# A state-space scan followed by hash-routed experts: squares, inter-chunk products and routing placed differently in the turns of the scan

## The chip, the cores and the metric

The kernel runs on one core of a Trainium2 chip. Its time is the device time of one launch in microseconds (us). The core has five instruction streams that run beside each other and meet at semaphores: TensorE (PE in the profile, with its weight loads as PEld), VectorE (DVE), ScalarE (ACT), GpSimd (POOL) and SyncE (SP), which here only issues DMAs.

## The reference

Two stages. The first is a state-space scan over 4 batches, 8 heads and 768 positions with head width 32 and state width 16. With `L[i, j]` the decay from position j to position i, a chunk gives

```python
CB = np.einsum('bhin,bhjn->bhij', Cc, Bc)
M = CB * L                                   # L is causal
y_intra = np.einsum('bhij,bhjd->bhid', M, xc)
y_inter = np.einsum('bhin,bhnd->bhid', Cc, state) * decay_to_i[:, :, :, None]
y[:, :, sl] = y_intra + y_inter
...
state = decay_full[:, :, None, None] * state + np.sum(Bx, axis=2)
```

`Bx` is the product of B and x, decayed to the chunk's end. The result is laid out as 3072 tokens of width 256. In the second stage each token goes to one of 8 experts, chosen by `token_ids * 2654435761 % 8`, and gets `relu(x @ w1[e]) @ w2[e]` with a hidden width of 1024.

## The kernel before

Everything is in fp32 except the small one-hot tables. The order of instructions on every engine is the order of the program text; a tile framework only adds the waits.

**The scan.** The kernel uses chunks of 64 positions. Two blocks of 128 positions make a pair; there are 3 pairs per batch and 12 pairs in all (`NP`), numbered `k`, with `b, j = divmod(k, 3)`. The main loop (L724) runs `k` from -1 to 11; a pass is called a turn here. A turn works on several pairs at once:

- *Rows* (`rows_part`, L203, called by `rows_due`, L707): POOL multiplies B or C of a batch by decay factors. A batch has 6 blocks of B rows and 6 of C rows.
- *Squares* (`turn_bc`, L214): TensorE transposes these 128x128 blocks into PSUM, four in a turn: B 0 to 3, then B 4, 5 and C 0, 1, then C 2 to 5 (`PARTS`, L212). `evict_bc` (L225) copies them out as `bt` (from B) and as `ct` and two masked forms `ce` (from C), nearly all on ACT.
- *Back* (`back`, L520; `evict_back`, L526): two blocks of `bt` for pair k+2 are turned back into `bn`.
- *States* (`states`, L543): DVE carries the state `z` through the four chunks of pair k+1; POOL scales each state into `sp` (L553).
- *Inter* (`inter`, L591): TensorE adds C times state to the output of pair k in PSUM (16 matmuls, 12 where the pair opens a batch); ACT copies the finished output to `y_sb` (L609), and `y_store` (L626) issues two DMAs to a DRAM buffer `y_tokens` on SP.
- *Gram* (`gram`, L566): C times B for pair k+2 into PSUM banks 0 to 3; `masked` (L578): DVE copies the causal part to `m_sb`, in two halves.
- *Intra* (`intra`, L611): the masked matrices times x for pair k+1; at its end ACT reads one column of the two output banks into `seen` (L622).
- *Dstates* (`dstates`, L530): B times x for pair k+2, into the other halves of banks 0 and 1, from where DVE's `z` reads them.

[...] `BT` = 6 and `BQ` = 7 take squares and back, `BY` = 4 and 5 the outputs.

**The routing.** In turns 0 to 8, `piece(k)` (L675) runs a part of the routing between gram and the masked copies: counts, ranks and slots of the tokens per expert, mostly small operations on DVE and POOL (`rt_...`, L269 to L426). In turn 6 and 7 one-hot `laneoh` rows are made (`rt_lanes`, L403), in turn 8 TensorE multiplies them by a table (`rt_table`, L419), into columns 256 on of bank `BQ`, and `to_index` (L428) makes the indices by which tokens are gathered.

**The experts.** POOL gathers tokens from `y_tokens` by indirect DMA (`gather`, L474) in tiles of 128; `turn_x` (L482) transposes a tile on TensorE and copies it to `xT`. The first tiles are gathered in turns 8 to 10, and two of them (`AHEAD`, L717) are transposed in turn 10 (L750). After the loop the experts run in pairs of halves with a Strassen-like scheme: `sums_x`, `sum_w1` and `sum_w2` form sums of tokens and weights on DVE, `up` (L844) and `down` (L907) are the matmuls, `put` (L942) transposes a result and scatters it to the output by indirect DMA on POOL. Four experts' first products are made (L979 to L1003) before the steps of L1090. Weights come by DMAs that SP issues, the first of them in turns 3 to 10 (`LOADS`, L720).

Of the kernel before, what the change touches and what calls it, by code (L numbers as in the profile page):

```python
# [9 lines left out]
F32 = mybir.dt.float32  # L10
# [15 lines left out]
def kernel(  # L26
# [187 lines left out]
    def turn_bc(b, part, bank):  # L214
        if part == 0:
            bts[b] = abat.tile([P, S], F32, name="bt")
            cts[b] = abat.tile([P, S], F32, name="ct")
            ces[b] = abat.tile([P, 2, S], F32, name="ce")
        k = 0
        for i, r0, r1 in PARTS[part]:  # L220
            for r in range(r0, r1):
                pe.transpose(out=ps[:, bank, k * P:(k + 1) * P], in_=rows[b, i][:, r], identity=ident)  # L222
                k += 1

    def evict_bc(b, part, bank, eng):  # L225
        k = 0
        for i, r0, r1 in PARTS[part]:
            src = ps[:, bank, k * P:(k + r1 - r0) * P].rearrange("q (r p) -> q p r", p=P)
            k += r1 - r0
            outs = [(bts[b], None, 0)] if i == 0 else [(ces[b][:, 0], 0, 1), (ces[b][:, 1], 1, 2), (cts[b], None, 3)]  # L230
            for o, e, n in outs:
                if n >= len(eng) or eng[n] is None:
                    continue
                o = o.rearrange("q (p r) -> q p r", r=R)[:, :, r0:r1]
                if eng[n] is act:
                    act.activation(o, src, AF.Copy, scale=1.0 if e is None else par[:, e:e + 1])  # L236
                elif e is None:
                    dve.tensor_copy(out=o, in_=src)
                else:
                    dve.tensor_scalar(out=o, in0=src, scalar1=par[:, e:e + 1], scalar2=None, op0=OP.mult)  # L240
# [84 lines left out]
    def rt_placed(pick, who):  # L325
        dve.tensor_reduce(out=sel, in_=pick, axis=AX.X, op=OP.add)
        whof = small("whof", [P, E])
        dve.tensor_reduce(out=whof, in_=who, axis=AX.X, op=OP.add)
        dve.tensor_copy(out=place_i, in_=whof)
# [9 lines left out]
    def rt_over_b():  # L339
        ov_i = small("ov_i", [P, E], I32)  # L340
        dve.tensor_scalar(out=ov_i, in0=ov, scalar1=0.0, scalar2=float(P - 1), op0=OP.max, op1=OP.add)
        dve.tensor_scalar(out=ov_i, in0=ov_i, scalar1=P.bit_length() - 1, scalar2=None, op0=OP.logical_shift_right)
# [82 lines left out]
    def rt_tabled():  # L425
        dve.tensor_copy(out=tabacc.rearrange("q i k -> q (i k)"), in_=ps[:, BQ, 2 * P:2 * P + 2 * NK])  # L426
# [753 lines left out]
```

## Time and profile before

| | |
|---|---|
| median of 3 timed runs | 247.5 us (247.07 to 250.94) |
| the profiled execution | 238.82 us |
| its span, first to last instruction | 237.1 us, mean granted TensorE clock 0.99 |
| busy share of the span | PE 94%, PEld 86%, DVE 72%, POOL 42%, ACT 41% |
| the scan ends: first expert matmul (L865) | 68.10 us |

The profile comes from one execution. The page gives busy time by engine, the chain of waits that ended last, and the costliest groups of instructions; the trace behind it can be asked for a timeline of one engine or for busy time in chosen windows. In a timeline, a line gives the start and the length in us, the engine, the source line, the operation, output and inputs, shapes, how many instructions are merged, and in brackets how long the engine idled before it and what released it. Where an instruction waited for several things, the trace names the one that came last by its records, which can be the wrong one. PEld overlaps PE: [...].

The page's slices (40 of equal length, busy share in tenths) show how the load shifts from the scan to the experts:

```profile
PE   7989999998899999999999999999999999999980
PEld 5777777777689897999999999999999999998960
DVE  6688887986526699989899797676758749537520
ACT  3647446642336632214223326434625533543220
POOL 2477879796855772004303532101430420310441
```

### The profile page before, as it was taken

The page shows a single profiled execution, that of the slowest core. Times are in us where ns is not written, and L with a number is a line of the kernel's source. Part 1 is how long each engine was busy: PE and PEld are TensorE (multiplying, and loading weights), DVE is VectorE, ACT ScalarE, POOL GpSimd, SP SyncE. Part 2 cuts the span into 40 slices and gives each one's busy share as a digit, 9 for nine tenths or more (in the row PEclk, how much of TensorE's full clock was granted, in tenths as well). Part 3 has the DMA queues.
Part 4 walks back from the last instruction along what each step waited for, and adds up shares of the span by engine and source line. Part 5 has one row for each costly group of instructions (what it writes and reads, how often), then busy time and mean ns, then how long its engine had stood idle before and what let it go on. Part 6 is the DMA issues. An engine that isn't in the chain of part 4 may idle for free.

```text
span 237.1 us, 6843 instructions
## 1 busy us (share of the span) xinstructions
PE 222.7 (94%) x2695; PEld 205.0 (86%) x2695; DVE 170.1 (72%) x351; ACT 97.2 (41%) x249; POOL 100.1 (42%) x177
## 2 busy tenths in 40 slices
PE   7989999998899999999999999999999999999980
PEld 5777777777689897999999999999999999998960
DVE  6688887986526699989899797676758749537520
ACT  3647446642336632214223326434625533543220
POOL 2477879796855772004303532101430420310441
PEclk9999999999999999999999999999999999999995
DMA  7988987887857999106607528306011400610111
GB/s 170 208 142 171 190 190 168 182 181 184 251 156 178 277 284 366 45 0 214 231 0 249 195 70 257 141 3 195 30 47 45 167 28 5 198 44 3 46 46 48
DMA packets 55174, 33.23 MB, mean 140 GB/s; under 512 B 34986, under 2 KB 49474, under 8 KB 55140
## 3 DMA queue, kind: packets, MB, share of 16 engines
q1 hardware_dynamic: 52288, 26.09, 42.4%
q0 software_dynamic: 2400, 6.43, 8.4%
q8 instruction: 22, 0.36, 0.6%
q10 hardware_dynamic: 452, 0.25, 0.4%
q14 instruction: 12, 0.10, 0.2%
HBM read 26.47 MB, written 6.42 MB: 139 GB/s over the span
## 4 chain that ended last, share of the span: by engine, by line
PE 44%; issue 31%; POOL 9%; DVE 7%; DMA 3%; ACT 3%; POOLq 1%; DVEq 0%; ACTq 0%
PE ps L865 12%; PE ps L924 10%; POOL out_dram L953 9%; PE ps L618 5%; PE ps L574 3%; PE ps L603 3%; PE ps L175 3%; PE ps L222 2%; DMA xg<-y_tokens,idx_in 2%; PE ps L538 2%; ACT ce L236 2%; PE ps L485 1%; DVE s L806 1%; DMA y_tokens<-y_sb 1%; DVE m L582 1%
## 5 line engine op out<-in xcount | busy, mean ns | idle before, releaser
L953 POOL DMA_INDIRECT out_dram<-o_sb,idx_out x25 | 29.7, 1190 | 73.8 <-ACT o_sb L949 71.5
L477 POOL DMA_INDIRECT xg<-y_tokens,idx_in x25 | 26.5, 1060 | 41.8 <-PE ps L944 30.4
L865 PE MATMUL ps<-t,s 128*128 128x202 f32 (+7 forms) x192 | 38.0, 328 | 0.6 <-DVE u L893 0.4
L924 PE MATMUL ps<-t,s 128*128 128x202 f32 (+7 forms) x192 | 35.2, 326 | 0.0
L865 PEld LDWEIGHTS ps<-t,s 128*128 128x128 f32 x192 | 32.0, 189 | 1.7 <-DVE u L893 0.9
L924 PEld LDWEIGHTS ps<-t,s 128*128 128x128 f32 x192 | 31.3, 189 | 0.0
L865 PE MATMUL ps<-xT,w 128*128 128x202 f32 (+7 forms) x128 | 25.3, 329 | 0.0
L806 DVE TENSOR_TENSOR s<-w 128x512 f32<-128x512 f32 x32 | 21.9, 684 | 0.2 <-DMA w<-in_moe_w_dram 0.2
L865 PEld LDWEIGHTS ps<-xT,w 128*128 128x128 f32 x128 | 21.0, 189 | 0.7 <-ACT p1e L876 0.5
L898 ACT ACTIVATE hx<-hx 128x404 f32<-128x404 f32 (+7 forms) x16 | 8.3, 525 | 31.2 <-DVE hx L897 31.2
L553 POOL TENSOR_TENSOR sp<-z,gm 128x128 f32<-128x128 f32 x44 | 17.9, 424 | 3.8 <-DVE z L561 1.9
L582 DVE COPY_PREDICATED m<-cmask,ps 128x512 f32<-128x512 int32 x24 | 16.2, 728 | 2.8 <-PE ps L574 2.7
L563 DVE SCALAR_TENSOR_TENSOR z<-z,g_sb,ps 128x128 f32<-128x128 f32 x40 | 13.9, 347 | 4.9 <-PE ps L538 1.1
L618 PEld LDWEIGHTS ps<-x_t,m 64*64 64x64 f32 x768 | 12.6, 134 | 2.5 <-ACT y_sb L609 1.2
L618 PE MATMUL ps<-x_t,m 64*64 64x64 f32 x768 | 14.3, 221 | 0.2
L930 ACT ACTIVATE d<-ps 128x202 f32<-128x202 f32 (+7 forms) x24 | 8.0, 331 | 14.0 <-PE ps L924 13.9
L865 PE MATMUL ps<-t,w 128*128 128x202 f32 (+7 forms) x64 | 13.2, 330 | 0.4
L865 PE MATMUL ps<-xT,s 128*128 128x202 f32 (+7 forms) x64 | 12.9, 326 | 0.0
L603 PE MATMUL ps<-sp,ct 64*64 64x128 f32 x176 | 12.2, 276 | 0.4 <-ACT seen L622 0.4
L924 PE MATMUL ps<-t,w 128*128 128x202 f32 (+8 forms) x72 | 12.4, 314 | 0.0
L924 PE MATMUL ps<-h,w 128*128 128x202 f32 (+7 forms) x64 | 11.8, 326 | 0.0
L865 PEld LDWEIGHTS ps<-t,w 128*128 128x128 f32 x64 | 10.7, 189 | 1.2 <-DVE hx L897 1.2
(176 smaller groups left out, 439.2 us busy)
## 6 DMA issues: line engine op xcount, KB each, us to landing
w<-in_moe_w_dram SPq DMA_DIRECT2D x8, 1024.0 KB, 5.8
w<-in_moe_w_dram SPq DMA_DIRECT2D x11, 512.0 KB, 6.9
x_t<-in_x_dram SPq DMA_DIRECT2D x24, 128.0 KB, 4.3
y_tokens<-y_sb SPq DMA_DIRECT2D x23, 128.0 KB, 3.5
w<-in_moe_w_dram SPq DMA_DIRECT2D x10, 256.0 KB, 3.7
bc<-in_B_dram SPq DMA_DIRECT2D x4, 384.0 KB, 4.9
bc<-in_C_dram SPq DMA_DIRECT2D x4, 384.0 KB, 5.4
xg<-y_tokens,idx_in POOLq DMA_INDIRECT x25, 4.9
```

What stands on the lines that cost most here:

```text
L477: pool_e.indirect_dma_start(out=xg[k], out_offset=None, in_=y_dram[0:n, :], in_offset=bass.IndirectOffsetOnAxis(ap=idx_in[:, k:k + 1], axi ...
L553: pool_e.tensor_tensor(out=sps[k][:, n].rearrange("q (h d) -> q h d", d=D), in0=zs["z"].rearrange("q (h d) -> q h d", d=D), in1=gm[:, un - ...
L563: dve.scalar_tensor_tensor(out=z, in0=zs["z"], scalar=g_sb[:, un - 1:un], in1=d, op0=OP.mult, op1=OP.add)
L582: dve.copy_predicated(out=m[:, :, g], mask=mk, data=ps[:, g, 0:2 * P].rearrange("q g (t s) -> q t g s", t=2))
L603: pe.matmul(out=y_own(r, u)[:, t], lhsT=cts[b][r, c:c + T], rhs=sps[k][r, n], start=False, stop=True, skip_group_check=True)
L618: pe.matmul(out=o, lhsT=m_sb[k % 2][u * T:(u + 1) * T, t, h // 2, (h % 2) * T:(h % 2 + 1) * T], rhs=xs[2 * k + t][u * T:(u + 1) * T, h // ...
L806: dve.tensor_tensor(out=t[:, i], in0=a, in1=b, op=op)
L865: pe.matmul(out=ps[:, bank, i * n:(i + 1) * n], lhsT=lhs[:, (q0 + i) * P:(q0 + i + 1) * P], rhs=rhs, start=((what in (1, 5) or what == (6 ...
L898: act.activation(hq(2), hq(2), AF.Relu)
L924: pe.matmul(out=src, lhsT=lhs(q), rhs=rhs(q)[:, c0:c1], start=((what in (1, 5) or alone) and q == 0), stop=True, skip_group_check=True)
L930: act.activation(st[what], src, AF.Copy)
L953: st = pool_e.indirect_dma_start(out=out[:], out_offset=bass.IndirectOffsetOnAxis(ap=idx, axis=0), in_=o_sb, in_offset=None, bounds_check= ...
```

## The change

1. **Squares.** From batch 2 on, a batch's six B squares are turned in one turn and its six C squares in the next (turns 2 and 3 for batch 2, 5 and 6 for batch 3), the last two of each six into bank `BQ`, columns 256 on; turns 4 and 7 turn none. Turns -1 to 1 are as before. The rows are made by POOL in the same turns as before. All copies stay on ACT (two of the prologue's stay on DVE); in turns 3 and 6 the C copies stand behind `bn`, one of them behind `seen`, and one in the next turn.
2. **Inter** of turns 2 to 11 moves to the front of the turn, before squares and back.
3. **AHEAD**: the two first token tiles are turned at the head of turn 11 instead of within turn 10, and DVE copies them instead of ACT.
4. **Scalings**: `sp` of pairs 10 and 11 is made on DVE, each before the next `z`, instead of on POOL.
5. **Table**: in bank `BT` instead of `BQ`, where `bn` comes from.
6. **Routing**: `rank_a`, `rank_b` and lanes 0 to 4 go behind the masked copies of their turns; lanes 21 to 23 go from POOL to DVE; the expert numbers come from the reduction directly, without a cast; the shift takes its count from a tile.
7. **sums_x(0)** is called one `up` earlier, ahead of `sum_w1`'s last piece.

```diff
-    def turn_bc(b, part, bank):
...
+    def turn_bc(b, i, r0, r1, bank, k=0):
...
+        for r in range(r0, r1):
+            pe.transpose(out=ps[:, bank, (k + r - r0) * P:(k + r - r0 + 1) * P], in_=rows[b, i][:, r], identity=ident)
+
+    def evict_bc(b, i, r0, r1, bank, k, eng, n=0):
+
+        src = ps[:, bank, k * P:(k + r1 - r0) * P].rearrange("q (r p) -> q p r", p=P)
+        o, e = (bts[b], None) if i == 0 else (cts[b], None) if n == 2 else (ces[b][:, n], n)
...
@@ rt_placed
-        whof = small("whof", [P, E])
-        dve.tensor_reduce(out=whof, in_=who, axis=AX.X, op=OP.add)
-        dve.tensor_copy(out=place_i, in_=whof)
+        with nc.allow_low_precision("whole numbers below 8"):
+            dve.tensor_reduce(out=place_i, in_=who, axis=AX.X, op=OP.add)
@@ rt_over_b
-        dve.tensor_scalar(out=ov_i, in0=ov_i, scalar1=P.bit_length() - 1, scalar2=None, op0=OP.logical_shift_right)
+        dve.tensor_tensor(out=ov_i, in0=ov_i, in1=shift_i, op=OP.logical_shift_right)
@@ rt_table (and the same in rt_tabled)
-        o = ps[:, BQ, 2 * P:2 * P + 2 * NK]
+        o = ps[:, BT, 0:2 * NK]
@@ states
-                pool_e.tensor_tensor(out=sps[k][:, n].rearrange("q (h d) -> q h d", d=D),
+                (pool_e if k < NP - 2 else dve).tensor_tensor(out=sps[k][:, n].rearrange("q (h d) -> q h d", d=D),
@@ piece
-            rt_rank_a()
...
-            rt_rank_b()
...
-            rt_lanes(0, 5, dve)
             rt_lanes(18, 21, pool_e)
...
-            rt_lanes(21, NCH, pool_e)
@@ before the main loop
+    SQUARES = {-1: [(1, 0, 0, 4, BY + 1, 0)], 0: [(1, 0, 4, 6, BT, 0), (1, 1, 0, 2, BT, 2)], 1: [(1, 1, 2, 6, BT, 0)]}
+    for b in range(2, NB):
+        SQUARES[3 * b - 4] = [(b, 0, 4, 6, BQ, 2), (b, 0, 0, 4, BT, 0)]
+        SQUARES[3 * b - 3] = [(b, 1, 4, 6, BQ, 2), (b, 1, 0, 4, BT, 0)]
@@ main loop
-        bt_, part = (b + 2, 0) if j == 2 else (b + 1, j + 1)
-        tb, qb, sb = (BY + 1, BY, BT) if k == -1 else (BT, BQ, 0)
-        if bt_ < NB:
-            turn_bc(bt_, part, tb)
+        qb, sb = (BY, BT) if k == -1 else (BQ, 0)
+        if k == NP - 1:
+            for i, q in enumerate(AHEAD):
+                turn_x(q, (BQ, BT)[i % 2], dve)
+        sq = SQUARES.get(k, ())
+        soon = k > 1
+        if soon:
+            inter(k)
+        for q in sq:
+            turn_bc(*q)
         if k + 2 < NP:
             back(k + 2, qb)
         if k + 1 < NP:
             states(k + 1, (0, 1), sb)
-        if bt_ < NB and part == 0:
-            evict_bc(bt_, part, tb, (act,))
-        elif bt_ < NB:
-            evict_bc(bt_, part, tb, (act, act, None if part == 1 else act, None))
+        for q in sq:
+            if q[1] == 0:
+                evict_bc(*q, act)
+            elif not soon:
+                evict_bc(*q, act, 0)
+                if k == 1:
+                    evict_bc(*q, act, 1)
         if k + 1 < NP:
             states(k + 1, (2, 3), sb)
-        if k == NP - 2:
-            for i, q in enumerate(AHEAD):
-                turn_x(q, (BQ, BT)[i % 2])
-        if k >= 0:
+        if not soon and k >= 0:
             inter(k)
         if k + 2 < NP:
             evict_back(k + 2, qb)
...
-        if bt_ < NB and part > 0:
-            evict_bc(bt_, part, tb, (None, None, act if part == 1 else None, act))
+        for q in sq:
+            if q[1] == 1:
+                for n in ((1, 2) if k == 0 else (2,) if k == 1 else (0, 1, 2) if q[4] == BQ else (0,)):
+                    evict_bc(*q, act, n)
+        if k - 1 in (3, 6):
+            evict_bc(*SQUARES[k - 1][1], act, 2)
...
         if k + 2 < NP:
             masked(k + 2, 0)
             masked(k + 2, 1)
+        if k == 1:
+            rt_rank_a()
+        if k == 3:
+            rt_rank_b()
         if k == 5:
             rt_slot_e()
+        if k == 6:
+            rt_lanes(0, 5, dve)
         if k == 7:
             rt_lanes(13, 18, dve)
+            rt_lanes(21, NCH, dve)
         if k + 1 < NP:
             intra(k + 1)
+        if k in (3, 6):
+            evict_bc(*sq[1], act, 1)
         if k + 2 < NP:
             dstates(k + 2)
...
@@ first products of the experts
+                if n == 15:
+                    sums_x(0)
...
     assert not turns
-    sums_x(0)
```

More of the change, by code (lines that the diff above doesn't have):

```diff
@@ L212 @@
     PARTS = [[(0, 0, 4)], [(0, 4, 6), (1, 0, 2)], [(1, 2, 6)]]
-    def turn_bc(b, part, bank):
[L215 to L240, printed above, removed]
+    def turn_bc(b, i, r0, r1, bank, k=0):
+        for d, e in ((bts, 1), (cts, 1), (ces, 2)):
+            if b not in d:
+                d[b] = abat.tile([P, S] if e == 1 else [P, 2, S], F32, name=("bt", "ct", "ce")[(bts, cts, ces).index(d)])
+        for r in range(r0, r1):
[3 more added lines that the diff above has]
+        o, e = (bts[b], None) if i == 0 else (cts[b], None) if n == 2 else (ces[b][:, n], n)
+        o = o.rearrange("q (p r) -> q p r", r=R)[:, :, r0:r1]
+        if eng is act:
+            act.activation(o, src, AF.Copy, scale=1.0 if e is None else par[:, e:e + 1])
+        elif e is None:
+            dve.tensor_copy(out=o, in_=src)
+        else:
+            dve.tensor_scalar(out=o, in0=src, scalar1=par[:, e:e + 1], scalar2=None, op0=OP.mult)
     sh = [P, E, NCH]
@@ L366, in rt_rank_b @@
                           in1=shift.unsqueeze(2).to_broadcast([P, E, NCH - EARLY]), op=OP.add)
+    shift_i = apre.tile([P, E], I32)
+    dve.memset(shift_i, P.bit_length() - 1)
     def rt_half2():
@@ L425, in rt_tabled @@
     def rt_tabled():
-        dve.tensor_copy(out=tabacc.rearrange("q i k -> q (i k)"), in_=ps[:, BQ, 2 * P:2 * P + 2 * NK])
+        dve.tensor_copy(out=tabacc.rearrange("q i k -> q (i k)"), in_=ps[:, BT, 0:2 * NK])
     def to_index(acc, o_in, o_out, n, tag, stack=apre):
@@ L648 @@
             pool_e.memset(ctab[:, i, p:p + 1], float(v))
-    turn_bc(0, 0, BT)
-    evict_bc(0, 0, BT, (act,))
+    turn_bc(0, 0, 0, 4, BT)
+    evict_bc(0, 0, 0, 4, BT, 0, act)
     filler(1)
-    turn_bc(0, 1, BY)
-    evict_bc(0, 1, BY, (act, act, dve, None))
-    turn_bc(0, 2, BY + 1)
-    evict_bc(0, 2, BY + 1, (None, act, dve, None))
+    turn_bc(0, 0, 4, 6, BY)
+    turn_bc(0, 1, 0, 2, BY, 2)
+    evict_bc(0, 0, 4, 6, BY, 0, act)
+    evict_bc(0, 1, 0, 2, BY, 2, act, 0)
+    evict_bc(0, 1, 0, 2, BY, 2, dve, 1)
+    turn_bc(0, 1, 2, 6, BY + 1)
+    evict_bc(0, 1, 2, 6, BY + 1, 0, act, 0)
+    evict_bc(0, 1, 2, 6, BY + 1, 0, dve, 1)
     o_dec, o_eid = ps[:, BQ, 2 * P:2 * P + NU], ps[:, BQ, 3 * P:3 * P + NCH]
@@ L663 @@
     rt_mask()
-    evict_bc(0, 1, BY, (None, None, None, act))
-    evict_bc(0, 2, BY + 1, (None, None, None, act))
+    evict_bc(0, 1, 0, 2, BY, 2, act, 2)
+    evict_bc(0, 1, 2, 6, BY + 1, 0, act, 2)
     gram(0)
```

## The prediction

> **What bounds the kernel now.** I read the page first, then the stages, then TensorE's weight loads turn by turn, then ACT and GpSimd where those loads waited. The windows by stage (window; length; busy us and instructions of PE, PEld, DVE, ACT, POOL; clock; DMA share; GB/s) say where time can be had at all:
>
> ```profile
> 13.60:25.90 12.30, 11.72 (x380) 9.40 (x380) 10.88 (x25) 7.07 (x20) 8.81 (x20) 1.00 0.87 168
> 39.30:52.80 13.50, 12.99 (x399) 10.54 (x395) 11.50 (x26) 7.79 (x21) 11.98 (x21) 1.00 0.85 177
> 52.80:68.10 15.30, 12.97 (x380) 10.19 (x377) 7.68 (x21) 4.46 (x14) 10.62 (x20) 1.00 0.70 192
> 95.00:215.00 120.00, 119.64 (x754) 118.39 (x753) 90.20 (x170) 46.10 (x116) 28.47 (x24) 1.00 0.32 106
> ```
>
> From 95 us on TensorE is full, and the diff does not touch that code. The state-space loop is what is edited; it ends with the first expert matmul at 68.10 us. There PEld, which shows the pace of the short matmuls better than PE, has holes. The timeline of weight loads (start, us, group, idle and releaser):
>
> ```profile
> 34.32 0.45 PEld L538 LDWEIGHTS ps<-x_t,bn 64*64 64x64 f32 x12 [0.62 <-ACT seen L622]
> 36.98 0.49 PEld L574 LDWEIGHTS ps<-ce,bt 32*64 32x64 f32 x32 [0.38 <-ACT ce L236]
> 39.28 0.42 PEld L222 LDWEIGHTS ps<-ident,rows 128*128 128x128 f32 x4 [0.17 <-issue]
> 39.67 0.25 PEld L524 LDWEIGHTS ps<-ident,bt 128*128 128x128 f32 x2
> 40.08 0.85 PEld L603 LDWEIGHTS ps<-sp,ct 64*64 64x64 f32 x16 [0.17 <-issue]
> 41.10 0.51 PEld L574 LDWEIGHTS ps<-ce,bt 32*64 32x64 f32 x32 [0.17 <-issue]
> 41.78 1.02 PEld L618 LDWEIGHTS ps<-x_t,m 64*64 64x64 f32 x64 [0.17 <-ACT y_sb L609]
> 42.81 0.46 PEld L538 LDWEIGHTS ps<-x_t,bn 64*64 64x64 f32 x16
> ...
> 63.56 0.20 PEld L485 LDWEIGHTS ps<-ident,xg 128*128 128x128 f32 x2 [1.18 <-DMA xg<-y_tokens,idx_in]
> 65.50 1.01 PEld L618 LDWEIGHTS ps<-x_t,m 64*64 64x64 f32 x60 [0.24 <-ACT y_sb L609]
> 67.05 0.88 PEld L603 LDWEIGHTS ps<-sp,ct 64*64 64x64 f32 x16 [0.53 <-issue]
> ```
>
> "Turn k" is the loop's value k. Lines 3 to 8 are turn 5 without a hole: squares 0.39, back 0.25, inter 0.85, gram 0.51, intra 1.02, dstates 0.45, and a 0.17 gap wherever the tile shape changes (128, 64, 32, 64, 128: four times). That is 4.15, and the next turn starts 4.16 later. With 12 inter matmuls (0.63) it would be 3.93, and turns 8 and 9 have no squares. The real starts of turns 1 to 10 are 21.22, 25.91, 30.20, 34.94, 39.28, 43.44, 48.12, 52.78, 58.04, 62.19. Against these costs, turns 3, 6, 7, 8, 9 lose about 0.8, 0.7, 0.5, 0.8, 0.6, turns 10 and 11 together 2.2, turn 1 loses 0.5, the rest 0.4: **6.5 us is about all that the loop can give**.
>
> The dstates wait at 34.32 is put on `seen`, but `seen` ended at 34.11. DVE's first masked copy (L582, started 33.53, 0.66 each) ended at 34.19: it reads the PSUM bank that dstates writes. The same lag of 0.13 to 0.17 fits at 16.59, 25.32 and 47.50. So routing work placed ahead of the masked copies on DVE delays TensorE.
>
> [...] The cast L329 took 0.64 for 8 elements and ended at 28.85, as POOL's rows ended at 28.82; the two-input L312 took 0.65 beside rows; the reduction L328 beside them took 0.21. [...]
>
> **The change, part by part.**
>
> *Inter first, turns 2 to 10.* The 64-wide intra, dstates and inter now follow each other: one tile-shape gap less, 9 x 0.17 = 1.5. But inter writes the columns that `seen` (ACT, after intra) reads, and `seen` is done about 0.56 after intra's last load (0.27 to reach ACT, 0.17, 0.12 back), while dstates covers 0.45: 0.1 a turn lost, net gain 0.6.
>
> *Squares in two turns of three.* The same 24 transposes at 0.10 and the same ACT copies; they go six at a time to turns 2, 3, 5, 6, and turns 4, 7 have none. The ce waits of 36.98 and 50.15 (0.2 each beyond the usual gap) go. Two things are late in their place.
>
> (a) GpSimd. Turn 5's squares read rows that rows_due makes in turn 4 behind rt_slot_b. Its timeline:
>
> ```profile
> 36.80 0.62 POOL L381 TENSOR_TENSOR val<-val,sel 128x192 f32<-128x192 f32 x1
> 37.38 0.50 POOL L382 TENSOR_TENSOR g<-g,sel 128x192 f32<-128x192 f32 x1
> 37.84 0.51 POOL L383 TENSOR_TENSOR g<-g,ovt 128x192 f32<-128x192 f32 x1
> 38.42 0.60 POOL L384 TENSOR_TENSOR g<-g,g 128x192 f32<-128x192 f32 x1
> 39.10 0.59 POOL L385 TENSOR_TENSOR val<-val,g 128x192 f32<-128x192 f32 x1
> 39.65 1.20 POOL L206 TENSOR_TENSOR rows<-bc,fac 128x256 f32<-128x256 f32 x2
> ```
>
> The first half of the rows stays at about 40.25. My turn 5 starts at 38.25 and wants squares at 39.27: **a wait of 1.1**, with back, gram and intra queued behind it. Turn 6's rows (43.15) come before their use (44.46).
>
> (b) ACT. In turns 3 and 6 the order is two y_sb, bn (behind back now), ce, ce, ct at 0.36, ce at 0.64, in turn 6 also tab16, then `seen`. Turn 6: bn starts 45.6, `seen` ends 48.7, and inter(7), ready at 47.9, **waits 1.0**; the rest of turn 7 is queued behind it. In turn 3 this ends at 34.3, about when the masked wait does.
>
> *Routing on DVE.* rank_a (0.79) goes behind the masked copies: turn 1's 0.35 wait goes. The reduction that writes place_i directly drops the 0.64 cast and 0.1 of turn 2's wait; SP's register loads only start sooner. rank_b (0.21) and lanes 0 to 4 (0.82) also go behind: turn 6's dstates wait (0.3 beyond the gap) goes, but lanes delay the next z by 0.6, covered by inter. The shift as a two-input op: [...] (0.95 in L342 before). From below its gain is 0, from above 0.6 (dstates of turn 3, and rt_past and so rows sooner). I take 0.
>
> *Table bank.* The table no longer waits for bn: 0.74 at 55.00 goes. Lanes 21 to 23 leave POOL (3 x 0.8) for DVE (0.5, from L409's 0.83 for 640); with lanes 13 to 18 they put z(9) at 53.85, so gram in turn 8 waits 0.5. Indices come at about 56.1 for 56.6. The gather also needs turn 7's y_store (issued 51.08 to 53.21, 3.5 to landing), so I move it by 0.3. No DMA is added; issues on SP stay in order at each turn's end.
>
> *Last states' scalings.* POOL loses 8 x 0.42; DVE gains 8 x about 0.28 (192 elements took 0.35 in L377) between the z (0.42 each). The chain of four grows from 1.7 to 2.7, and gram of turn 9, already released by z at 60.03, ends at 60.65 for 60.60: the earlier start of turn 9 is eaten.
>
> *First squares of tokens, turn 10 to 11.* The gathers' 1.18 wait and `seen`'s 0.4 before the last inter are covered by other work; two DVE copies (0.42) replace ACT's before the last y_sb. Turn 10 starts 62.4, intra ends 65.06, two squares, inter 65.6, first expert matmul **66.6 for 68.10**.
>
> *sums_x(0) one call sooner.* It waits for ACT's xT at 79.77 either way; sum_w1's 0.68 moves behind it, before v5 at 82.32. Zero; if that cover went, 0.7.
>
> My starts after: 25.5, 29.8, 34.5, 38.25, 43.65, 48.85, 52.55, 57.55, 62.4 for turns 2 to 10. **Sum: 1.5 us earlier**, carried through a TensorE-bound rest. Against the profiled execution's 238.8 (span 237.1) that is 237.3. The median shown is 247.5, 8.7 above that execution, which the trace does not explain; I subtract from it: **246.0**.
>
> **The rivals.** *No new waits:* ACT and GpSimd run with more slack than I charge; (a), (b) and turn 8's wait (2.6) drop out, and the shift's 0.6 comes: 4.7 gained, 242.8. For it: both engines have idle time (ACT 7.8 of 13.5). Against: POOL is busy 12.0 of the same 13.5. Chance 0.33, in half of which a little more tips it over 2%. *Absorbed:* weights or gathers do not come sooner (DMA share 0.89 from 68 to 95 us) and the gain is spent there: 247.5, chance 0.12. *Slower, GpSimd becomes the bound:* [...] From 1.3 us of stretch, turn 6's squares wait too; at 1.5 the gain is gone; at 3 in turn 5 and a further 1.7 in turn 6, 249.2. Against: the moved ops sum to about 2.4 in turns 3 to 7, most not beside rows. Chance 0.13. My case: 0.42.
>
> **The numbers.** 246.0. The range takes rival one with 1 us more at the fast end, and the slower one with the spread of the runs (247.07 to 250.94) at the other: 241.8 to 249.6. Two per cent is 4.95 us, about what a measurement of this kernel can tell from no change. Faster by that: 0.23 (half of rival one's 0.33, and 0.06 for my own case with terms mis-sized), slower: 0.08 (the far end of the last rival), within: 0.69.
>
> **What would show it.** First expert matmul near 66.6; L538 waits of turns 1 and 6, the table's and the gather's waits gone; a squares wait near 1.1 on POOL rows in turn 5; inter waiting about 1.0 for `seen` in turn 7; gram waiting for z in turn 9. I am wrong if these waits are absent, or if 66.6 holds and the end does not follow.

## The result, and the profile after

| | before | after |
|---|---|---|
| median, first set of runs | 248.44 us (244.47 to 253.73, 22 runs) | 246.5 us (242.19 to 249.37, 22 runs) |
| ratio to before | | 0.9885, 95% interval 0.9836 to 0.9934 |
| the profiled execution | 238.82 us, clock 0.99 | 242.59 us, clock 0.986 |
| its span | 237.1 us | 240.9 us |
| first expert matmul | 68.10 us | 69.37 us |

The forecast was 246.0. By the 2% bound this counts as no change; the interval puts the change at 1.6% to 0.7% faster. The ratio leaves out executions more than 1.5% above the fastest of their kernel, so it can differ from the ratio of the medians. The two profiled executions say the opposite of the medians: the one of the changed kernel is 3.8 us longer. So the first thing to find is what that one execution lost.

TensorE's weight loads in the changed kernel, turns 4 to 9, only the lines that start a turn or follow a wait (start, length in us, group, idle before it and its releaser):

```profile
34.19 0.95 PEld L596 LDWEIGHTS ps<-sp,ct 64*64 64x64 f32 x15
38.07 0.88 PEld L596 LDWEIGHTS ps<-sp,ct 64*64 64x64 f32 x16 [0.17 <-POOL g L376]
39.89 0.64 PEld L219 LDWEIGHTS ps<-ident,rows 128*128 128x128 f32 x6 [0.94 <-POOL rows L206]
43.14 0.66 PEld L596 LDWEIGHTS ps<-sp,ct 64*64 64x64 f32 x12
47.95 0.88 PEld L596 LDWEIGHTS ps<-sp,ct 64*64 64x64 f32 x16 [0.80 <-issue]
51.59 0.88 PEld L596 LDWEIGHTS ps<-sp,ct 64*64 64x64 f32 x16
56.65 0.66 PEld L596 LDWEIGHTS ps<-sp,ct 64*64 64x64 f32 x12 [0.18 <-issue]
58.91 0.42 PEld L567 LDWEIGHTS ps<-ce,bt 32*64 32x64 f32 x14 [0.40 <-DVE z L556]
```

L596 is inter, now the first group of its turn, and so marks the turn's start (turn 4's first load, recorded by itself, stands at 34.14). The wait for rows in turn 5, the wait before inter in turn 7 and the wait for z in turn 9 are the forecast's. The two ce waits and the dstates wait for `seen` in turn 6 are gone. Up to 59.5 us the scan is ahead of the kernel before: turn 9 starts at 56.65 for 58.04.

Then it loses it. The same view from turn 9's intra (L611) on:

```profile
59.50 1.05 PEld L611 LDWEIGHTS ps<-x_t,m 64*64 64x64 f32 x49 [0.17 <-issue]
61.01 0.22 PEld L611 LDWEIGHTS ps<-x_t,m 64*64 64x64 f32 x5 [0.47 <-issue]
61.77 0.19 PEld L611 LDWEIGHTS ps<-x_t,m 64*64 64x64 f32 x3 [0.54 <-issue]
62.49 0.21 PEld L611 LDWEIGHTS ps<-x_t,m 64*64 64x64 f32 x3 [0.54 <-issue]
63.24 0.21 PEld L611 LDWEIGHTS ps<-x_t,m 64*64 64x64 f32 x4 [0.53 <-issue]
63.33 0.72 PEld L531 LDWEIGHTS ps<-x_t,bn 64*64 64x64 f32 x12
63.94 1.75 PEld L596 LDWEIGHTS ps<-sp,ct 64*64 64x64 f32 x16
```

Four times TensorE stands for about half a microsecond, 2.08 together, and the trace shows nothing that it waits for ("issue"). Behind that, the same groups take longer: inter 1.75 for 0.88, dstates 0.72 for 0.45. The windows around it (window; length; busy us of PE, PEld, DVE, ACT, POOL with instructions; granted clock; DMA share; GB/s) say why:

```profile
60.50:63.00 2.50, 1.18 (x24) 0.66 (x15) 1.16 (x3) 0.00 (x0) 1.93 (x2) 1.00 0.85 261
63.00:66.50 3.50, 3.07 (x37) 2.84 (x36) 1.74 (x6) 0.92 (x3) 1.22 (x2) 0.56 0.83 254
67.00:69.37 2.37, 2.37 (x76) 1.96 (x65) 0.76 (x2) 0.49 (x2) 0.66 (x2) 1.00 0.53 126
```

A lull at full clock, then a clock of 0.56, then full clock again. The slow clock adds 0.27 on dstates, 0.87 to 0.90 on inter, and about 0.3 on the start of turn 10's intra. Without lull and slow clock the first expert matmul would stand near 65.8 (69.37 - 2.08 - 1.5), 2.3 us ahead of the kernel before. This is an estimate on the low side: the few loads between the pieces are slow too, and the whole intra took 3.95 us (59.50 to 63.45) where it takes 1.02 elsewhere. With that in its place the estimate is near 65. A further 2.5 us went behind it: from the first expert matmul to the end took 171.5 us, for 169.0 before, with waits of 0.84 and 1.29 between 79 and 89 us.

### The profile page after: what moved, and what is told of

It is laid out like the page before. It is cut to its first block, busy times and chain, and to the rows that moved or that the text cites. A ratio compares the mean times of both kernels' runs of the same rounds, so it can differ in the third digit from the quotient of the medians.

```text
span 240.9 us, 6827 instructions
## 1 busy us (share of the span) xinstructions
PE 224.1 (93%) x2695; PEld 207.0 (86%) x2695; DVE 172.6 (72%) x362; ACT 96.8 (40%) x247; POOL 94.3 (39%) x166
## 4 chain that ended last, share of the span: by engine, by line
PE 40%; issue 33%; POOL 13%; DVE 9%; ACT 2%; POOLq 1%; DVEq 0%; ACTq 0%
PE ps L882 12%; POOL out_dram L970 10%; PE ps L941 8%; PE ps L611 4%; PE ps L596 3%; PE ps L567 3%; PE ps L478 2%; PE ps L531 2%; PE ps L219 2%; DVE z L556 2%; ACT ce L227 1%; DVE m L575 1%; DVE s L823 1%; DVE m L144 1%; PE ps L517 1%
## 5 line engine op out<-in xcount | busy, mean ns | idle before, releaser
L970 POOL DMA_INDIRECT out_dram<-o_sb,idx_out x25 | 28.9, 1155 | 78.6 <-ACT o_sb L966 70.2
L611 PE MATMUL ps<-x_t,m 64*64 64x64 f32 x768 | 16.1, 223 | 1.8 <-issue 1.5
L611 PEld LDWEIGHTS ps<-x_t,m 64*64 64x64 f32 x768 | 13.6, 136 | 4.6 <-issue 3.1
L546 POOL TENSOR_TENSOR sp<-z,gm 128x128 f32<-128x128 f32 x36 | 14.9, 425 | 5.2 <-DVE z L554 3.2
L596 PE MATMUL ps<-sp,ct 64*64 64x128 f32 x176 | 13.4, 287 | 0.6 <-ACT seen L615 0.6
L596 PEld LDWEIGHTS ps<-sp,ct 64*64 64x64 f32 x176 | 10.6, 141 | 1.9 <-issue 1.3
L602 ACT ACTIVATE y_sb<-ps 128x256 f32<-128x256 f32 x23 | 8.7, 384 | 8.4 <-PE ps L596 7.0
```

What stands on the lines that cost most here:

```text
L546: (pool_e if k < NP - 2 else dve).tensor_tensor(out=sps[k][:, n].rearrange("q (h d) -> q h d", d=D), in0=zs["z"].rearrange("q (h d) -> q h ...
L596: pe.matmul(out=y_own(r, u)[:, t], lhsT=cts[b][r, c:c + T], rhs=sps[k][r, n], start=False, stop=True, skip_group_check=True)
L602: act.activation(o[:, u], y_own(slice(0, P), u), AF.Copy)
L611: pe.matmul(out=o, lhsT=m_sb[k % 2][u * T:(u + 1) * T, t, h // 2, (h % 2) * T:(h % 2 + 1) * T], rhs=xs[2 * k + t][u * T:(u + 1) * T, h // ...
L970: st = pool_e.indirect_dma_start(out=out[:], out_offset=bass.IndirectOffsetOnAxis(ap=idx, axis=0), in_=o_sb, in_offset=None, bounds_check= ...
```

## The experiments

**One: the changed kernel again, beside the kernel before run again as a program of its own, and each of two parts alone.** No edit in the first two:

> The changed kernel once more. My theory: the scan's gain is real and the stretch of its first profile (intra of turn 9 taking 4 us from 59.5 us, then TensorE at half clock) belongs to that execution, not to the change. Then turn 9 starts near 56.6 us again, the first expert matmul comes at 64.8 to 65.8 us, and the ratio to the kernel before is 0.985 to 0.992. Rival: the change brings the stretch about (late gathers, crowded DMA queues), so intra of turn 9 takes over 3 us again and the first expert matmul comes at 68 to 70 us.

Measured: 239.4 us (22 runs) for 240.05 (59 runs), ratio 0.9979 (0.9947 to 1.001). The profiled execution has span 236.7, the first expert matmul at 67.61 and no slow clock ahead of it (1.00 from 40.12 to 67.61); from there to the end 169.1 us. Its loads:

```profile
29.69 0.83 PEld L611 LDWEIGHTS ps<-x_t,m 64*64 64x64 f32 x49 [0.80 <-issue]
38.68 0.84 PEld L611 LDWEIGHTS ps<-x_t,m 64*64 64x64 f32 x51 [0.72 <-issue]
41.17 0.64 PEld L219 LDWEIGHTS ps<-ident,rows 128*128 128x128 f32 x6 [0.17 <-POOL rows L206]
52.04 0.19 PEld L567 LDWEIGHTS ps<-ce,bt 32*64 32x64 f32 x4 [0.86 <-issue]
```

Three gaps inside groups, 2.38 us, at other places than in the first execution. The wait for rows in turn 5 is gone, since TensorE comes 2 us later and POOL doesn't. Less its gaps, the first expert matmul would stand at 65.2 (with the rows' wait back, nearer 66), about as in the first execution. The stretch in turn 9 did not come, as the theory has it, but the first expert matmul and the ratio fell short of its 64.8 to 65.8 and 0.985 to 0.992: the gaps had not been foreseen.

> The kernel before, as a run of its own: what two profiles of one program differ by, and the floor of the timing. My theory: the turns start where they did (turn 5 at 39.3, turn 9 at 58.0, first expert matmul at 68.1 us, each within 0.5), unless a stretch without TensorE instructions falls into the scan; the ratio is 1.00 within 0.006. If such stretches are the ordinary thing, this profile shows one somewhere and its span is above 240 us, as the timed runs' 248 against the first profile's 238.8 suggest. Rival: the timed runs are slower for a reason that no profile shows, and the span is 237 again.

Measured: 244.1 us (6 runs), ratio 1.0157 (1.0078 to 1.0237) to the runs of the same program. Its profiled execution waits 3.02 us for the second token tile in turn 10, and then has a clock of 0.51 from 68.20 to 72.73:

```profile
66.50 0.20 PEld L485 LDWEIGHTS ps<-ident,xg 128*128 128x128 f32 x2 [3.02 <-DMA xg<-y_tokens,idx_in]
70.80 1.60 PEld L603 LDWEIGHTS ps<-sp,ct 64*64 64x64 f32 x16 [0.58 <-issue]
72.73 1.17 PEld L865 LDWEIGHTS ps<-xT,w 128*128 128x128 f32 x4 [0.33 <-issue]
```

So one program differed from itself by 1.6% here, with six runs on one side; a later set of 22 runs gave 0.9986 (below). The tile that was 1.18 us late in the execution that the forecast was read from can be 3 us late.

```diff
 (the kernel before)
+        if k > 1:
+            inter(k)
         if bt_ < NB:
             turn_bc(bt_, part, tb)
...
-        if k >= 0:
+        if 0 <= k <= 1:
             inter(k)
```

> The kernel before with inter first in turns 2 to 10 and nothing else. My theory: one tile-shape gap less a turn (9 x 0.17), 0.1 a turn back to the wait for seen, so 0.6 gained; but ACT now copies y_sb before ce, and gram of turns 4 and 7 comes right behind squares and back, so it waits for ce about 1.1 us instead of 0.4 in each. First expert matmul at 68.6 to 69.4 us: no gain alone. Rival: ce is ready early enough and the gaps count in full: 66.6 to 67.5 us.

Measured: 239.94 us, ratio 1.0004 (0.9977 to 1.003), first expert matmul at 69.32, of which 0.70 is a gap in turn 10's intra (66.71) of the kind that Three deals with. Inter first shows no gain by itself. With all the C squares of a batch still in one turn, gram waits for `ce` in turns 4 and 7, 1.39 us each, where it waited 0.38 before:

```profile
38.89 0.49 PEld L574 LDWEIGHTS ps<-ce,bt 32*64 32x64 f32 x32 [1.39 <-ACT ce L236]
52.85 0.49 PEld L574 LDWEIGHTS ps<-ce,bt 32*64 32x64 f32 x32 [1.39 <-ACT ce L236]
```

Inter had stood between the squares and gram, and covered ACT's copies. With the squares regrouped, the changed kernel's loads show no wait for `ce` in these turns. The regrouping is what makes inter first possible, and the parts of the change don't add up one by one; the regrouping was not run by itself.

The routing moves and the table's bank alone (rank, `place_i`, lanes 0 to 4 and 21 to 23, table to `BT`):

> The kernel before with the routing moves and the table's bank alone (rank_a, rank_b, lanes, place_i without a cast; the shift as it was). My theory: dstates waits of turns 1 and 6 and the table's wait go (0.35, 0.3, 0.74), so turn 9 starts at 56.5 to 57.0 us instead of 58.04; but the token tiles turned in turn 10 wait for gathers, which wait for turn 7's stores, so most of it is lost there and the first expert matmul comes at 67.3 to 68.1 us. Rival: the gathers follow the indices, and all of it arrives: 66.6 to 67.0 us.

Measured: 239.33 us, ratio 0.9986 (0.9955 to 1.0017). The profiled execution waits 2.83 us for the second token tile and has its first expert matmul at 73.28, so it cannot price them. By the ratio's interval the routing alone lies between 0.5% faster and 0.2% slower.

**Two: two parts undone, and the new waits mended.** On this occasion the kernel before took 250.36 us (58 runs).

> The changed kernel once more, beside the next three. Theory (the turn starts are as forecast, and what differs from one execution to the next are the stretches of 0.5 to 1.0 us [...]): starts of turns 2 to 5 within 0.5 us of 25.5, 29.8, 34.2, 38.1 plus the gaps named 'issue' inside matmul groups; first expert matmul 65.0 plus those gaps, so 66 to 68.5; ratio to before 0.990 to 0.998. Rival (the first comparison's 0.9885 is what the change brings, and the second one's 0.998 was the odd one): ratio 0.989 or lower.

Measured: 246.84 us, ratio 0.999 (0.9947 to 1.0032). Turns 4 to 9 start at 35.09, 38.96, 44.03, 48.85, 52.49, 57.54, all 0.9 after the first execution, and the lull in turn 9 and the slow clock come again at the same place (TensorE busy for 1.68 of the 3.50 us from 61.00, a clock of 0.50 from about 65.0 to 68.5): first expert matmul 70.59, later than the 66 to 68.5 of the theory; the ratio is neither the theory's 0.990 to 0.998 nor the rival's. So the stretch in turn 9 is no matter of one execution. From the first expert matmul to the end it took 175.1 us. The waits lie between 80 and 92 us:

```profile
80.77 0.63 PEld L882 LDWEIGHTS ps<-xT,w 128*128 128x128 f32 x4 [0.98 <-issue]
89.59 0.20 PEld L478 LDWEIGHTS ps<-ident,xg 128*128 128x128 f32 x2 [1.50 <-issue]
91.97 1.17 PEld L882 LDWEIGHTS ps<-t,s 128*128 128x128 f32 x5 [2.17 <-DVE u L910]
```

In the 25 us from 70 us on the DMA queues moved 221 GB/s here. In the 25 us from 68 us on they moved 263 in the execution of 236.7 and 261 in the kernel before's of 237.1. Slower supply to the experts goes with the longer end; why it was slower no run shows.

```diff
-                (pool_e if k < NP - 2 else dve).tensor_tensor(out=sps[k][:, n]...
+                pool_e.tensor_tensor(out=sps[k][:, n]...
```

> The changed kernel with the scalings of the last two turns' states back on GpSimd. Theory (the forecast's): the eight scalings were worth nothing, since they eat on VectorE what they free on GpSimd: the gram wait for z of 0.40 in turn 9 goes, and the scalings of turn 10 now stand behind three gathers on GpSimd, ending 62.4 to 63.0 where the gathers start near 57.6, so that the inter matmuls of turn 10 (63.2 in an execution with 3 us of gaps) do not wait; first expert matmul within 0.5 us of the changed kernel's. Rival (the gathers hold them up): where the first gather starts at 58.9 the scalings end 64.2 or later, inter of turn 10 waits 1 us or more, and the median is 1 to 2.5 us above the changed kernel's.

Measured: 247.91 us, ratio 0.9857 (0.9817 to 0.9897). The gathers started late, at 60.26, and still the scalings that stand behind them ended at 65.62, before inter of turn 10 came at 66.59 (after its own gaps, at a clock of 0.50 from about 65.2). The wait for z in turn 9 is gone. So in this execution the scalings set nothing; but inter was late by over 4 us of gaps and slow clock. The scalings ended 5.36 us after the first gather started. From the changed kernel's first gather, 58.85 in its first execution and 57.58 in its second, that makes 64.2 and 62.9 (an estimate), and inter of turn 10 would stand near 61.6 without gaps. There it would wait 1.3 us or more, as the rival says. The median and the ratio point to opposite sides of the changed kernel's. What the scalings are worth stays open.

```diff
-        if k == NP - 1:
-            for i, q in enumerate(AHEAD):
-                turn_x(q, (BQ, BT)[i % 2], dve)
...
+        if k == NP - 2:
+            for i, q in enumerate(AHEAD):
+                turn_x(q, (BQ, BT)[i % 2])
         for q in sq:
```

> The changed kernel with the squares of the first two token tiles back in turn 10, copied by ScalarE. Theory: they wait for the gathers as in the kernel before (1.18 there, 3.02 and 2.83 in two later executions) and inter and intra of turn 10 stand behind them on TensorE's queue; TensorE waits 1.0 to 3.0 us for the gathered tokens, first expert matmul 1 to 2.5 us later than in the changed kernel beside it, median 1 to 2.5 us higher. Rival (the wait is covered: what is not waited for in turn 10 is waited for at the first expert matmuls): first expert matmul and median within 0.5 us of the changed kernel's.

Measured: 246.96 us (6 runs), ratio 0.9881 (0.9802 to 0.9961), first expert matmul 68.89. My theory missed: the squares came at 65.76 without a wait. In this kernel they stand behind inter, not ahead of it as in the kernel before. But that does not show that the move to turn 11 is needless. By its landing records the second tile was there at 65.51, only 0.4 us before its squares at 65.93, and TensorE was late: gaps of 0.40, 0.41, 0.57 and 0.86 and a clock of 0.50 from about 61.8 to 65.2 lie ahead, and inter started at 64.16 for about 61.6 without such losses. By this estimate the squares would have come ahead of the tile in a scan without them. Whether the turn or the order within it takes the gather off TensorE's path stays open.

```diff
+    def rt_tiles_b():
         act.activation(tab16[:, :, 1], toh, AF.Copy, scale=iota_p[:, 0:1])
...
-        if k != 4:
-            rows_due(k + 2)
+        rows_due(k + 2)
...
-        if k == 4:
-            rows_due(k + 2)
...
         if k in (3, 6):
             evict_bc(*sq[1], act, 1)
+        if k == 7:
+            rt_tiles_b()
```

> The changed kernel with its two new waits mended: the rows of turn 4 on GpSimd ahead of the slots' first part, and ScalarE's half of the tile table (tab16) behind the eviction of the seen states one turn later. Theory (the waits are real and on the path): no wait of TensorE for rows in turn 5 (0.94 in the first profile of the changed kernel), the inter wait of turn 7 from 0.80 to 0.25 or less; 1.0 to 1.4 us off the start of turn 8, first expert matmul 1.0 earlier for the same sum of 'issue' gaps, median 0.7 to 1.4 us below the changed kernel's. Rival (the next thing is late instead: slots 1.2 us later on GpSimd put the table, and so the gathers, later, or an instruction gap stands where the wait stood): waits gone, first expert matmul and median within 0.5 us.

Measured: 246.89 us, ratio 0.9875 (0.9821 to 0.9929). Both waits are gone: the squares of turn 5 follow inter at once, and inter of turn 7 starts at 48.52 with an idle of 0.19. Yet turns 4 to 9 take 22.45 us (35.50 to 57.95), as they do in the third execution without the mending (35.09 to 57.54). VectorE and TensorE in turn 7:

```profile
48.52 0.88 PEld L598 LDWEIGHTS ps<-sp,ct 64*64 64x64 f32 x16 [0.19 <-issue]
49.94 0.92 PEld L569 LDWEIGHTS ps<-ce,bt 32*64 32x64 f32 x32 [0.17 <-issue]
50.30 1.41 DVE L402 TENSOR_TENSOR laneoh<-iota,where 128x1024 bf16<-128x1024 f32 x1
51.63 1.34 DVE L577 COPY_PREDICATED m<-cmask,ps 128x512 f32<-128x512 int32 x2
52.43 0.46 PEld L533 LDWEIGHTS ps<-x_t,bn 64*64 64x64 f32 x16 [0.37 <-issue]
```

Gram took 0.92 for 0.48, and dstates waits 0.37 behind the masked copies, which the 1.41 us of lanes hold up on VectorE. In turn 5, too, dstates now waits 0.54 us, where it did not. The rival was right by the trace: the waits were real, but the next thing was late in their place. The medians are 0.05 us apart (246.89 and 246.84); the ratios, 0.9875 and 0.999, would make the mended kernel 1.1% better, as much as two sets of the changed kernel differ (0.9885 and 0.999). No version here beats the changed kernel by more than that.

**Three: where the gaps and the slow clock lie.** In every execution so far I counted TensorE's records (weight loads, matmuls and its few others) from the start up to the end of each gap. Those of 0.4 us and more that lie inside a group, or where the named engine had long been done:

| execution | count at the gap's end (us lost) |
|---|---|
| changed, second | 1217 (0.80), 1730 (0.72), 2497 (0.86) |
| before, second | 1218 (0.93), 3009 (1.13, named z) |
| inter alone | 1473 (1.05), 3265 (0.70) |
| routing alone | 705 (0.62), 961 (0.49), 2753 (0.86), 3009 (1.28, named z) |
| scalings on GpSimd | 1217 (1.62), 1730 (0.46), 2753 (1.02), 3009 (1.23) |
| tokens in turn 10 | 1986 (0.40), 2242 (0.41), 2753 (0.57), 3009 (0.86) |
| both mended | 1217 (1.07) |

All are 193 or 194 more than a multiple of 256. At the two marked "named z" the trace puts the wait down to VectorE's `z`, but that had ended 0.20 and 0.35 us before, where 0.05 is usual. The other long waits for an engine lie at other counts. The first and third executions of the changed kernel have no such gap over 0.4. To move that count against the program:

```diff
-        for _ in range(2 * n):
-            pe.matmul(out=ps[:, bank, 0:2 * P], lhsT=fill16[:, 0:P], rhs=fill16[:, 0:2 * P], ...)
+        for _ in range(n):
+            pe.matmul(out=ps[:, bank, 0:4 * P], lhsT=fill16[:, 0:P], rhs=fill16[:, 0:4 * P], ...)
```

> The changed kernel with half as many filler matmuls at the start, each twice as wide (36 TensorE records fewer ahead of the loop, the same columns). In the runs so far the stretches in which TensorE waits for nothing that the trace shows, outside waits for an engine, lie where the count of TensorE's records from the start (weight loads and matmuls, with its own few others) is 193 more than a multiple of 256: 961, 1217, 1473, 1730, 2242, 2497, 2753, 3009. Theory [...]: they stay at these counts, and so fall 36 records later in the program, some 18 weight loads further on; their sum between 18 and 60 us stays 1 to 3 us, and time and turn starts stay within the spread of the changed kernel. Rival (they belong to the place in the program, for instance to what the DMA queues carry then): they stay at the same weight loads, at counts 36 lower.

Measured: gaps at 704 (1.13), 960 (0.88), 1216 (1.65) and 1729 (2.14), and ahead of the stretch forecast one at 449 (1.35).

```profile
33.65 0.56 PEld L611 LDWEIGHTS ps<-x_t,m 64*64 64x64 f32 x32 [1.65 <-issue]
44.04 0.60 PEld L611 LDWEIGHTS ps<-x_t,m 64*64 64x64 f32 x34 [2.14 <-issue]
```

The counts stayed (192 or 193 more than a multiple of 256, one fewer than above), the place moved: the gap at 1216 leaves 32 loads of intra where it left 49, the one at 1729 leaves 34 where it left 51. That is a shift of 17 loads, where the theory has some 18. The sum of the four, though, was 5.8 us instead of 1 to 3, and the kernel ran 242.94 us, ratio 1.0055 (1.0017 to 1.0094). How large the gaps are I did not foresee, only where.

> The kernel before, once more, beside the others: what one set of runs of an unchanged program differs from another. Theory: ratio to the shared runs of before anywhere from 0.99 to 1.02, as the second set gave 1.016; in its profile the second token tile is waited for in turn 10 for 1 to 3 us, [...]. Rival (a set repeats within 0.3%): ratio 0.997 to 1.003, and the second set's 1.016 was chance of six runs.

Measured: 243.26 us (22 runs) for 240.29 (75 runs of the same program), ratio 0.9986 (0.9946 to 1.0025). By the ratio the rival is right and a set repeats, by the medians it differs by 1.2%. The profiled execution, span 237.1, had gaps of 0.54, 0.74 and 0.64 in the scan and then waited only 0.45 for the tile, not 1 to 3; its first expert matmul stands at 68.18, where the first execution, with no such gap and a wait of 1.18, has 68.10. In these two executions the tile's landing (63.56, 63.64) sets the end of the scan, and gaps ahead of it are hidden. In others it comes later (66.50 in the second execution); whether gaps put it off there, no run shows.

```diff
         if k == NP - 2:
+            filler(10)
             for i, q in enumerate(AHEAD):
```

> The kernel before with 20 filler matmuls (128x256, about 2.1 us at full clock) ahead of the first two token tiles' squares in turn 10, so that TensorE works where it waited for the gathers. Theory (the fall of the clock follows TensorE's lull): granted clock 1.00 from 60 to 75 us; against an execution of the kernel before with a 3 us wait and the half clock behind it, first expert matmul 1.5 to 2.5 us earlier (about 70.5 for 72.7), against one with a 1.2 us wait 0.9 later; median 0.5 to 2 us under the kernel before on a chip where most executions are long. Rival (the fall of the clock has nothing to do with the lull, [...]): the half clock comes all the same, first expert matmul 72 to 74.

Measured: 241.31 us, ratio 1.0052 (1.002 to 1.0083). TensorE stood a further 1.63 us behind the fillers, and kept its clock (loads with the last filler's matmul, then the windows around the wait):

```profile
63.76 2.08 PEld L175 LDWEIGHTS <-fill 128*128 128x128 bf16 x20 [0.17 <-issue]
67.47 0.27 PE L175 MATMUL ps<-fill 128*128 128x256 bf16 x1 [1.46 <-issue]
67.48 0.47 PEld L485 LDWEIGHTS ps<-ident,xg 128*128 128x128 f32 x4 [1.63 <-issue]
```

```profile
65.84:67.48 1.64, 0.18 (x3) 0.01 (x2) 0.00 (x0) 0.00 (x0) 1.53 (x5) 1.00 0.92 332
67.48:72.28 4.80, 4.22 (x102) 3.40 (x101) 0.00 (x0) 1.93 (x6) 0.57 (x2) 1.00 0.28 74
```

The 1.63 us are not what they seem. The last filler's matmul needs no token, and it too began only at 67.47; the count there is 3266, 194 more than a multiple of 256. So this is a gap of the kind above. The second tile's landing record stands at 67.39, just ahead of its end, so without the gap TensorE would have waited about as long for the tile, and without gap and fillers about 3.5 us (63.9 to 67.4, an estimate). The clock is as the theory says, 1.00 up to 76 us, in this one execution; the first expert matmul, at 72.28, not 70.5, is not. The tile came 0.9 later than in the second execution of the kernel before (66.46); from its landing to the first expert matmul it took 4.9 us at a clock of 1.00, for 6.3 there, of which 4.5 at 0.51. By this estimate the kept clock saved some 1.4 us in this execution. Over the runs, by the ratio's interval, the fillers cost 0.2 to 0.8% more than they save; their 2.1 us are spent whether or not there is a wait.

```diff
-        if soon:
-            inter(k)
         for q in sq:
...
-        if not soon and k >= 0:
+        if k >= 0:
             inter(k)
```

> The changed kernel with the inter matmuls of turns 2 to 10 back behind the squares, back and the z chain's second half; all else stays. Theory (inter first is worth 0.6 net of its waits for seen, and in turn 7, where tab16 stands ahead of seen, costs 0.8): the wait of turn 7 for seen goes, a second gap of 0.17 in each of nine turns comes; turn lengths in turns 2 to 6 and 8 to 9 0.1 longer, turn 7 0.5 shorter, starts of turn 10 and first expert matmul within 0.7 us of the changed kernel's, median likewise. Rival (inter first carries the gain): first expert matmul 1.5 us later or more.

Measured: 239.86 us, ratio 0.9991 (0.9957 to 1.0024). Turn 10's inter starts at 62.37 with no gap at the counts above before it, for about 61.6 in the first execution of the changed kernel less its lull and the slow dstates. First expert matmul 69.97, after a gap of 1.71 at count 3266 and 3.2 us at clock 0.50. Less these it would be near 67, 1 to 2 us behind the changed kernel's 65 to 65.8: it leans to the rival, though the medians show nothing of it. Two details went against me. The wait of turn 7 for `seen` stayed (0.71). And the squares of turn 5 wait 1.87 instead of 0.94, because inter no longer stands in front of them:

```profile
39.91 0.64 PEld L219 LDWEIGHTS ps<-ident,rows 128*128 128x128 f32 x6 [1.87 <-POOL rows L206]
```

## Why the prediction was right

**The starts.** Forecast for turns 2 to 9: 25.5, 29.8, 34.5, 38.25, 43.65, 48.85, 52.55, 57.55. The first execution has 25.47, 29.77, 34.14, 38.07, 43.14, 47.95, 51.59, 56.65. Up to turn 5 they agree within 0.4, which fits what was put down for the routing moves of turns 1 and 2; then the new waits were charged too high. (One reading behind it was slightly off: the masked copy ahead of the dstates wait at 34.32 ended at 34.25, not 34.19, as it took 0.72. The conclusion holds, with a lag of 0.07.)

**(a) GpSimd's rows, 1.1 forecast, 0.77 measured** (0.94 less the usual 0.17). GpSimd kept its pace:

```profile
38.66 0.59 POOL L378 TENSOR_TENSOR val<-val,g 128x192 f32<-128x192 f32 x1
39.21 1.20 POOL L206 TENSOR_TENSOR rows<-bc,fac 128x256 f32<-128x256 f32 x2
```

They start 0.44 sooner than before, and TensorE's turn 0.2 sooner than I had it. For the slower rival these instructions show no sign: the first took 0.59 and the rows 1.20, as long as in the kernel before.

**(b) `seen` behind ScalarE's evictions, 1.0 forecast, 0.6 to 0.8 measured.** ScalarE in turn 6:

```profile
45.10 0.38 ACT L521 ACTIVATE bn<-ps 128x256 f32<-128x256 f32 x1 [0.64 <-PE ps L517]
45.38 0.86 ACT L227 ACTIVATE ce<-ps,par 128x256 f32<-128x256 f32 x2
46.97 0.81 ACT L410 ACTIVATE tab<-toh,iota 128x600 bf16<-128x600 bf16 x1
47.66 0.18 ACT L615 ACTIVATE seen<-ps 128x2 f32<-128x2 f32 x1
```

I had summed the durations. The starts lie closer: bn takes 0.38 and the next begins 0.28 later, tab16 takes 0.81 and `seen` begins 0.69 later. The queue ends at 47.84 where I had 48.7; of the 0.86, 0.5 is the earlier start. That ScalarE's instructions overlap in the records is what the sum left out.

**z behind the lanes in turn 8, 0.5 forecast, 0.8 measured.** The bracket shows only 0.27, but gram's 32 loads are spread over 1.28 us (53.62 to 54.90) where they take 0.48 unhindered. The second part starts at 54.48, as the last z ends at 54.43:

```profile
53.62 0.60 PEld L567 LDWEIGHTS ps<-ce,bt 32*64 32x64 f32 x18
54.48 0.42 PEld L567 LDWEIGHTS ps<-ce,bt 32*64 32x64 f32 x14 [0.27 <-DVE z L556]
```

**z in turn 9** is waited for, as forecast, but the term behind it was the largest that was mis-sized. With the scalings on VectorE the chain of four z was to grow from 1.7 to 2.7 us, and gram to end 0.05 later than before, so that turn 9's earlier start would be eaten. The chain took 2.1 us (56.76 to 58.86), and gram's loads ended at 59.33 for 60.45, so 1.1 us of it were kept. **The shift as a two-input operation** gains nothing, as taken: it took 0.95 and ended at 32.74, as GpSimd's rows ended at 32.72. In the kernel before it took 0.95 too and ended at 33.07, the rows at 33.05.

**The table and the gathers.** The table's wait is gone. But the first gather starts at 58.85, not 0.3 sooner than 57.04: it waits for turn 7's `y_store`, which SP issued at 53.13 for 51.08, behind its issues for `x_t` (51.19 to 53.04). The forecast of the gathers failed here. It cost nothing, since the tiles are now asked for behind turn 10's intra, in turn 11. The forecast had called the gathers' 1.18 "covered": in none of the three executions of the changed kernel does TensorE wait for these tiles.

**The sum.** Forecast: first expert matmul at 66.6 for 68.10. Less gaps and slow clock it is near 65 to 65.8 (first) and 65.2 to 66 (second execution), so by this estimate 2 to 3 us of gain were made in the scan, not 1.5. Of this the gaps take a part that I had not in the sum at all. The profiled execution of before happened to have none, and in its third execution, with 1.9 us of them, they vanish in the wait for the tile. The changed kernel has no such wait and pays each in full: 67.61 in the second execution, with 2.38 us of them, is 0.5 better than 68.10. Three sets gave 0.9885, 0.9979 and 0.999, that is 2.8, 0.5 and 0.2 us; the forecast's 1.5 of 247.5 is 0.994. It lies among them, just outside the interval of each. By the medians of all runs the three sets give 1.9, 0.7 and 3.5 us. The waits were of the right kind and in the right places, but that 246.5 came so near to 246.0 is luck: waits were charged some 0.9 too high up to turn 9 and the z chain more on top, gaps and slow clock were not charged, and the kernel before itself took 248.44 in this set and not 247.5. How large the true gain is, between nothing and about 1%, stays open: the changed kernel's ratio moved by 1% from set to set, and the kernel before's against itself by up to 1.6%.

**The unexplained 8.7 us** between profiled execution and median: the traces of longer executions hold candidates for its parts. They are gaps of up to 5.8 us in sum, a clock of 0.50 for 3.4 or 6.8 us (worth up to half that, an estimate), a tile that lands 3 us late, and up to 6 us between 80 and 92 us where the experts wait. The last was seen in the changed kernel and its variants alone. No execution of the kernel before as long as its median of 247.5 was traced, so which of these made up its 8.7 us is not shown. The rival *Absorbed* is not refuted where the experts wait so; *No new waits* is refuted, since (a) and (b) are in the trace. `sums_x(0)` and the shift were not tried by themselves.

## What to carry to other kernels

Where a group is moved to the front, ask what it used to cover behind it: inter first cost 1 us at each gram until the squares were regrouped, and hides half of the wait for rows now. A wait for a landing hides the delays ahead of it, as long as they don't put off the landing itself; once the wait is gone, those delays count. And a variant that removes a wait proves little if its own execution came late for another reason: look at how far ahead the awaited thing was there. Before a trace's stalls are summed, look at a second execution of the same program: half a per cent of gain needs more than one.

## What the runs showed of the hardware

*Gaps at fixed counts.* The gaps end where TensorE's records reach 192 to 194 more than a multiple of 256, and with 37 records fewer ahead of the loop they kept their counts and so moved in the program. The trace also has transfers of 16 KB on a queue that it names "instruction": 22 in an execution with some 5480 records of TensorE, about one for each 256. For the gap that ended at 29.69 in the second execution of the changed kernel, the traffic from 26.60 to 28.40 includes:

```profile
q1 hardware_dynamic: 1125, 0.48, 94.2%
q8 instruction: 1, 0.02, 6.0%
```

6.0% of 16 engines over 1.8 us is one engine for 1.7 us, beside data at 94%; the shortest such transfer in the first executions of both kernels took 0.88. There are 31 gaps of 0.4 us and more at such counts in the 12 later executions, and in each TensorE went on 1.2 to 1.7 us after the end of the last such transfer. The timing and the shift would fit a late transfer as the cause, but no run changed the transfers themselves, so the cause was not shown. The longest of these gaps took 2.14 us.

*The slow clock.* In the 14 traces the granted clock falls to 0.50 for 3.41 or 6.83 us at a time, and the stretches of full clock are multiples of 3.41 us too (58.03 ahead of the fall and 170.67 behind it in the first execution of the changed kernel, 225.28 in that of the kernel before). So I took, for each fall, how long TensorE stood in the 3.41 us ahead of it. In the first execution of the changed kernel (windows as above):

```profile
60.03:63.44 3.41, 1.86 (x48) 1.26 (x45) 1.50 (x3) 0.00 (x0) 2.10 (x3) 1.00 0.90 250
63.44:66.85 3.41, 3.13 (x46) 2.91 (x45) 1.74 (x6) 0.94 (x3) 1.22 (x2) 0.50 0.80 253
```

TensorE stood for 1.55 of the 3.41 us ahead of the fall. Of the 12 falls between 15 and 95 us, ten came behind a stretch in which it stood for 1.55 to 2.59 us; two, among the pieces of turn 9's intra, behind 1.06 and 0.94. A stretch with 1.66 us (tokens in turn 10, from 82.29) had no fall behind it. Nor had two lulls between weight loads, of 2.23 us (the same execution) and 1.87 us (inter behind the squares). So these traces give no sharp threshold, and the length of a lull alone does not decide.

*Open:* the two to five pieces of about half a microsecond in turn 9's intra lie at counts of 3107 to 3189, not at those of the gaps above. They came in five of the eight executions of the changed kernel and its variants, and in none of the six of the kernel before and its variants. So they may be a cost of the change, and then "less lull and slow clock" above flatters it. But all five are from the two sets in which the kernel before took 248 and 250 us; the three without pieces, and all traced executions of the kernel before but its first, are from sets in which it took 240; that first one, from a set of 247.5, has no pieces. What the pieces are was not found.
